# A hand-ordered attention-and-MLP kernel gets a new written order for all five engines

## Chip, cores and metric

The kernel runs on one core of a Trainium2 chip. The metric is the device time of one execution in microseconds (us). Five instruction streams run side by side and wait for each other through semaphores: TensorE (PE, matrix products and transposes), VectorE (DVE), ScalarE (ACT), GpSimd (POOL), and SyncE (SP, which only issues transfers). Each stream executes its instructions strictly in the order in which they were written.

## What is computed

Attention with four sink keys and a window of 128 keys, then a two-layer MLP with a sigmoid-gated activation:

```python
def _attn_ref(q, k, v, n_sink, window):           # (4, 8, 768, 64), n_sink 4, window 128
    scores = 1.0 / np.sqrt(D) * np.matmul(q, k.transpose(0, 1, 3, 2))
    rel = pos[:, None] - pos[None, :]
    keep = (pos[None, :] < n_sink) | ((rel >= 0) & (rel < window))
    scores = np.where(keep, scores, -1e9)
    a = np.exp(scores - np.max(scores, axis=-1, keepdims=True))
    return np.matmul(a / (np.sum(a, axis=-1, keepdims=True) + 1e-09), v)

def _moe_ref(x, w_in, w_out):                     # x (3072, 512), d_ff 2048
    h = x @ w_in
    return (h * (1.0 / (1.0 + np.exp(-1.702 * h)))) @ w_out
```

## The kernel before

The 4 x 768 queries are cut into 24 blocks of 128 tokens (all 8 heads at once). They are worked in the list ORD: first the four blocks that begin a batch (0, 6, 12, 18), which look only at their own keys, then the other twenty. "Place n" below is the position in that list: places 0 to 3 are the batch beginnings, places 4 to 23 the rest. Two places make a pair, and a pair (256 tokens) goes through the MLP together.

One place runs through these steps:

- load q, k and v of the block (lines 298 and 289). POOL issues these transfers, which also cast to 16 bits, in one queue that all loads share with the MLP weights: w_in in four quarters (line 307) and w_out in four quarters (line 316);
- transpose q and k: at places 0 to 7 by PE against the identity (line 391), evacuated by DVE or ACT; at later pairs by a DMA transpose that SP issues (line 412);
- scores on PE: at places 0 to 3 a mask is first written into PSUM by a product of the identity with `bias0` (line 438) and the scores are added (line 446); at places 4 to 7 own and previous block apart (line 446); from place 8 on both in one step (line 471). Scores against the four sinks go to `misc` (line 490), from `ksb`, the transposed sink keys;
- DVE packs own and previous block into one row of 128 keys per head (line 514), takes the maximum (526, 542, 545), subtracts (583, 598); ACT takes the exponential into `a` (616, or 569 straight out of PSUM);
- transpose `a` into `at`: at places 0 to 3 by PE (line 679), at places 4 to 23 by a DMA transpose from SP (line 717). Then POOL splits `at` by two selects: `atp`, the keys of the previous block (line 628), and `at` itself, the keys of the own block (line 622);
- values on PE (lines 738, 744, 748; two halves per place). The product with the sinks takes `vsb`, which is made once per batch out of the sink values `vsa` (a small load by SP, line 341) by a product on DVE or POOL (line 346);
- normalise on DVE into `xn` (759, 760), transpose into `xT`: at places 0 to 7 by PE (line 773), later by one DMA transpose per pair (line 786);
- MLP of the pair: eight first steps hT (line 808, eight products of 256 columns each; pair 0 in two halves of its own), the activation on ACT (838), eight second steps o (line 859, four products of 512 columns), evacuation by ACT or DVE (271, 267) and the store by SP (877).

While it waits at the beginning, PE runs products of a zero tile into `misc` (line 888). How many stand ahead of which step is said in `FILL`.

The body of the kernel only makes a list of 922 numbered operations ("plan"). The string `ORDER` then says in which order they are emitted and on which engine (P, V, A, G, S for PE, DVE, ACT, POOL, SP), and `HOME` in which ring of PSUM buffers a score, value or MLP tile lives. Costs and dependencies given to `plan.add` are notes for the search that wrote the order; the emission does not read them. What an instruction waits for follows from the data that it touches and from the buffers that it takes:

```python
    with tc.manual_schedule():
        for item in ORDER:
            op = plan.ops[int(item[:-1])]
            for n in range(FILL.get(op.seq, 0)):
                nc.tensor.matmul(misc[:, 256:512], fill[:, 0:P], fill, start=True, stop=True)
            op.emit(engines[item[-1]]) if op.many else op.emit()
```

A load on POOL has one more wait: the loads share eight semaphores in turn, so the ninth load after another is issued when that other one has landed.

Operations that are named below, by their number (the same in both kernels):

| number | what |
|---|---|
| 0, 1; 20, 21 | loads of q and k of place 0 as f32 (line 220, from SP and ACT); their casts |
| 3, 5 | the selects that make the identity (line 225) and the mask `bias0` (line 233), on POOL |
| 22 to 29 | loads of q, k, v for places 0 to 3 |
| 12 | the zeroing of `vsb` on DVE (line 251) |
| 108, 110, 114 | transposes of q and of k, scores, of place 0 |
| 580 to 595 | first steps of pair 0 |
| 101, 100, 102, 103; 104 to 107 | the loads of `vsa` for batches 1, 0, 2, 3; the products `vsb` for batches 0 to 3 |
| 236, 237, 238 and 240 | place 5: DMA transpose of `a`, the two selects, the two halves of values |
| 212, 213, 214 and 216 | the same of place 4 |
| 260, 261, 262 and 264 | the same of place 6 |
| 281 | second half of the subtraction of place 7 |
| 321, 322, 325 and 323 | the same of place 9; 310 are its scores |
| 327, 696 | the DMA transpose xT of places 8 and 9; the first MLP step that reads it |
| 357, 358, 361 | place 11: transpose, selects, first half of values |

Of the kernel before, what the change touches and what calls it, by code (L numbers as in the profile page):

```python
# [40 lines left out]
9V 2V 18V 16V 4V 13V 19V 17V 12V 23G 0S 1S 7S 22G 28G 29G 3G 15V 11V 26G 21A 20V 108P 109V 110P 5G 10V 113P 27G 132P  # L41
133A 111V 112V 114P 130P 116V 32G 24G 25G 36G 37G 131A 118A 115V 31G 117V 174P 135P 136P 137V 119A 122P 175A 176P
139V 120P 138V 121V 152P 177A 154P 179P 33G 180P 123V 153A 141A 142P 155A 140A 35G 157P 182V 181V 184A 30G 41G 40G
124P 158P 183V 185A 159V 161V 126P 143A 34G 163A 144P 160V 127V 186P 162A 145V 187V 125V 164P 188P 146P 198P 189V
147V 165A 128P 129A 148P 149V 190P 191V 168P 196P 197A 192P 166P 150P 199A 582P 193V 194P 167V 169V 170P 151A 202P
590P 171V 583A 46G 47G 50G 49G 172P 173V 586P 594P 195A 178A 39G 38G 620P 591A 587A 595A 201P 200P 222P 612P 6S 203V
220P 221A 621A 614P 613A 615A 204V 223V 205V 206V 14V 207V 134V 208V 210V 608P 588P 592P 609A 589A 593A 209V 42G 43G
52G 55G 53G 584P 246P 618P 247V 585A 8S 101S 105G 48G 56G 45G 244P 270P 245V 225P 271V 224P 228V 610P 226P 619A 268P
580P 44G 616P 269A 581A 230V 227V 229V 231V 233V 622P 617A 232V 234V 248P 249P 251V 252V 253V 596P 623A 611A 235A
# [3 lines left out]
67G 65G 61G 285G 646P 294P 296V 295V 263V 297V 647A 265V 298V 299V 636P 640P 650P 300V 301V 302V 651A 648P 649A 644P  # L53
637A 645A 638P 642P 641A 639A 59G 266P 286P 288P 643A 267V 287V 289V 303A 652P 310P 312V 313V 653P 290P 57G 86G 54G
64G 68G 291A 304S 658P 314V 315V 311P 659P 328S 316V 674P 319V 318V 660P 317V 320A 676P 661P 664P 678P 677A 675A
321S 305G 71G 364S 662A 654P 73G 329P 665A 679A 102S 331V 322G 333V 655P 668P 669A 332V 308P 334V 672P 95G 309V 330P
325P 673A 74G 335V 306P 326V 666P 70G 323P 336V 337V 667A 670P 324V 307V 63G 79G 686P 671A 338V 327S 346P 339A 687P
680P 688P 347P 348V 349V 351V 350V 656A 340S 352V 353V 106G 681P 629S 355V 354V 689P 696P 356A 690A 382P 341G 60G
697A 657S 357S 384V 385V 682P 383P 692P 683P 386V 80G 693A 400S 103S 387V 388V 389V 390V 698P 694P 699A 78G 365P
695A 684A 702P 367V 358G 369V 704P 368V 370V 391V 705A 703A 700P 344P 366P 69G 76G 66G 77G 345V 371V 701A 361P 708P  # L60
392A 362V 359P 373V 714P 360V 342P 706P 393S 343V 372V 709P 715P 374V 363S 375A 418P 685S 707A 716P 376S 420V 394G
422V 710P 421V 436S 156A 717P 423V 419P 711P 718V 424V 425V 427V 722P 663S 712A 426V 83G 720P 726P 401P 723A 721A
728P 403V 724P 402P 729A 405V 377G 107V 75G 404V 725A 406V 730P 731A 72G 82G 88G 81G 397P 398V 407V 395P 732P 733A
727A 380P 734P 742P 396V 90G 408V 410V 428A 381V 378P 379V 736P 399S 743P 409V 411A 737P 735A 412S 454P 744P 456V
429S 738P 457V 713S 455P 739P 745P 458V 459V 89G 85G 472S 460V 413G 746A 462V 461V 748P 463V 437P 749A 754P 439V
752P 755A 430G 92G 414P 753A 740A 415V 440V 442V 441V 438P 758P 762P 750P 416P 443V 84G 96G 91G 94G 445V 433P 759A
756P 417V 444V 434V 751A 763A 770P 757A 464A 431P 764P 760P 432V 446V 435S 741S 490P 447A 765P 761A 448S 491P 766P
493V 492V 494V 495V 771P 465S 496V 499V 767P 768A 508S 691S 778P 769S 449G 497V 772P 779A 498V 788P 473P 789A 466G
784P 785A 475V 476V 474P 773P 477V 478V 479V 87G 98G 99G 452P 780P 781A 482V 774A 776P 467P 790P 97G 468V 481V 782P
791A 453V 777A 480V 469P 450P 786P 451V 470V 798P 787A 471S 775S 783A 526P 500A 792P 529V 528V 799P 527P 531V 530V  # L70
793P 483A 501S 532V 800P 533V 535V 794P 484S 534V 536A 806P 795P 807A 537S 502G 509P 801P 544S 511V 485G 802V 513V
796A 512V 510P 808P 505P 809A 810P 514V 747S 818P 811A 93G 506V 486P 538G 804P 487V 503P 805A 812P 816P 504V 813A
819A 515V 516V 517V 488P 814P 826P 489V 507S 815A 817A 562P 518V 519A 565V 564V 820P 827P 563P 520S 567V 566V 568V
828P 821P 571V 569V 829P 834P 570V 572A 545P 822P 830V 521G 835A 803S 831S 842P 573S 547V 548V 823P 843A 550V 549V
524P 824A 832P 546P 551V 554V 553V 846P 574G 525V 838P 847A 833A 552V 539P 540V 541P 840P 542V 844P 839A 841A 577P
836P 837A 848P 522P 523V 555A 854P 543S 849P 855P 845A 556S 850P 719S 797S 856P 575P 851P 557G 868P 576V 852A 857P
853S 869A 862P 858A 860P 870P 560P 861A 561V 863A 578V 866P 864P 871A 558P 865A 872P 559V 867A 882P 873A 876P 825S
579S 883P 877P 874P 878P 875A 884P 879P 892P 880V 885P 881S 893A 894P 886V 888P 887S 895A 859S 890P 889A 898P 891A
896P 899A 902P 910P 897A 900P 903A 911P 901A 904P 912P 905P 916P 906P 917P 907P 913P 908V 918P 914A 919P 909S 915S
920A 921S  # L80
# [9 lines left out]
HOME = dict(x.split(":") for x in "0:own 2:pv 6:own 8:own 10:pv 12:own 16:own 17:own 19:pv 20:pv 22:mm 25:own 26:own 27:mm 28:mm 29:own 32:pv 35:pv 38:own 39:pv 41:pv 43:own 45:own 46:mm 49:mm 50:mm 52:mm 53:mm 54:own 56:pv 57:mm 59:own 60:mm 61:mm 62:mm 64:own 66:mm 67:own 69:own 70:mm 168:own 170:pv 173:pv 174:own 177:pv 178:pv 179:pv 181:own 183:own 185:pv 187:pv 188:pv 191:pv 192:own 195:pv 197:pv 203:pv 204:own".split())  # L90
# [60 lines left out]
def kernel(  # L151
# [123 lines left out]
    late = []  # L275
# [8 lines left out]
    def load_one(which, b, key, after, deps):  # L284
# [7 lines left out]
        if b in CFG["f32"]:  # L292
# [3 lines left out]
            )  # L296
        return sw(
            key, 0.88, lambda: nc.gpsimd.dma_start(buf()[:, i, w], src), 0.9,  # L298
            take=[buf], after=after, deps=deps,
        )  # L300

    for g in range(NG):
# [622 lines left out]
```

## Time and profile before

| what | us |
|---|---|
| median of 3 runs | 230.03 (230.0 to 230.13) |
| the profiled execution: its time | 229.54 |
| the profiled execution: its span, from the first to the last instruction | 227.8 |
| PE busy | 216.8 |
| DVE, ACT, POOL busy | 136.0, 127.3, 114.3 |

A row of a timeline gives the start in us, the duration in us, the engine, the line, the operation, what is written and read, and how many such instructions in a row are merged; in brackets the idle time of the engine before it and what ended it. SPq rows are the issue of a transfer, not the transfer. PE is pipelined: the duration of a row holds some 0.2 us of the last product's way through the array, so that the cost of a step is read from start to start. In the table of stretches each engine has its busy time and its number of instructions.

### The profile page before, as it was taken

To read this page: it belongs to the slowest core of one execution; us is meant where nothing else is said; L and a number is where in the kernel's file an instruction comes from. 1 tells how busy PE (TensorE), PEld (TensorE's weight loads), DVE (VectorE), ACT (ScalarE), POOL (GpSimd) and SP (SyncE) were. 2 spreads that over 40 slices of the span, in tenths; PEclk is the share of its full clock that TensorE was granted. 3 is DMA by queue.
4 is the path that set the end of the run, shared out by engine and by line. 5 is a ranking of instruction groups with operands and counts; after the bars stand their busy time and mean duration, and the time that the engine had idled before them with its cause. 6 is when DMAs were issued, how large, how long until landed. Compare 5 with 4: busy or idle time off the path is not lost.

```text
span 227.8 us, 5439 instructions
## 1 busy us (share of the span) xinstructions
PE 216.8 (95%) x2237; PEld 153.0 (67%) x2237; DVE 136.0 (60%) x334; ACT 127.3 (56%) x196; POOL 114.3 (50%) x126
## 2 busy tenths in 40 slices
PE   6789999996999999899999999999999999999994
PEld 4568998444785684585685695685695695775862
DVE  5799389674858188576875876577587751131101
ACT  2689675711584836757539359347646738441621
POOL 7995575118994594692794490570570430300000
PEclk9999999999999999999999999999999999999999
DMA  9999999999999999999999999998982703620302
GB/s 134 148 159 204 181 187 206 168 142 228 175 108 143 217 116 141 202 166 112 241 148 149 223 97 171 195 147 125 183 138 54 192 0 71 214 42 7 138 0 92
DMA packets 131992, 32.82 MB, mean 144 GB/s; under 512 B 124640, under 2 KB 129024, under 8 KB 131968
## 3 DMA queue, kind: packets, MB, share of 16 engines
q0 software_dynamic: 77024, 13.37, 77.6%
q1 hardware_dynamic: 53904, 18.85, 41.2%
q10 hardware_dynamic: 1040, 0.26, 0.5%
q8 instruction: 17, 0.28, 0.5%
q14 instruction: 7, 0.06, 0.1%
HBM read 27.36 MB, written 6.29 MB: 148 GB/s over the span
## 4 chain that ended last, share of the span: by engine, by line
PE 62%; DMA 16%; POOL 11%; issue 6%; DVE 1%; ACT 1%; POOLq 0%; SPq 0%
PE hT L808 28%; PE o L859 25%; DMA w_out<-in_moe_w_out_dram 6%; DMA w_in<-in_moe_w_in_dram 5%; POOL qkn L298 3%; DMA xT<-xn 3%; DMA at<-a 3%; POOL at L622 3%; POOL atp L628 2%; POOL v L289 2%; PE own L471 2%; PE av L744 2%; PE av L748 2%; PE av L738 1%; PE prv L471 1%
## 5 line engine op out<-in xcount | busy, mean ns | idle before, releaser
L808 PE MATMUL hT<-xT,w_in 128*128 128x256 f16 (+1 forms) x832 | 93.3, 264 | 0.9 <-DMA xT<-xn 0.9
L859 PE MATMUL o<-w_out,gT 128*128 128x512 f16 (+1 forms) x400 | 91.0, 371 | 0.0
L808 PEld LDWEIGHTS <-w_in 128*128 128x128 f16 x832 | 73.6, 98 | 13.0 <-DMA xT<-xn 1.4
L838 ACT ACTIVATE gT<-hT 128x512 f16<-128x512 f32 x96 | 54.7, 599 | 49.4 <-PE hT L808 49.0
L859 PEld LDWEIGHTS <-gT 128*128 128x128 f16 x400 | 36.8, 98 | 33.8 <-ACT gT L838 0.2
L628 POOL TENSOR_SCALAR_AFFINE_SELECT atp<-at 128x1024 f16<-128x1024 f16 x20 | 22.0, 1098 | 70.2 <-DMA at<-a 59.4
L514 DVE COPY_PREDICATED own<-later,prv 128x512 f32<-128x512 uint16 x40 | 26.5, 692 | 30.8 <-PE prv L471 25.9
L616 ACT ACTIVATE a<-e 128x1056 f16<-128x1056 f32 (+1 forms) x24 | 24.1, 1014 | 16.9 <-DVE e L598 7.1
L526 DVE TENSOR_REDUCE mx<-own 128x4 f32<-128x512 f32 x48 | 31.7, 685 | 1.6 <-PE own L446 1.1
L583 DVE TENSOR_TENSOR e<-own,mx 128x512 f32<-128x512 f32 x44 | 29.2, 684 | 0.8
L289 POOL DMA_DIRECT2D v<-in_v_dram x24 | 21.5, 899 | 3.3 <-DMA w_out<-in_moe_w_out_dram 3.3
L622 POOL TENSOR_SCALAR_AFFINE_SELECT at<-at 128x1024 f16<-128x1024 f16 x20 | 22.2, 1110 | 1.4
L298 POOL DMA_DIRECT2D qkn<-in_q_dram x23 | 20.7, 904 | 2.1 <-DMA w_in<-in_moe_w_in_dram 1.6
L298 POOL DMA_DIRECT2D qkn<-in_k_dram x23 | 20.8, 906 | 1.7 <-POOLq L906 0.8
L760 DVE TENSOR_TENSOR xn<-av,rcp 128x256 f16<-128x256 f32 x48 | 20.4, 425 | 1.7
L271 ACT COPY osb<-o 128x512 f32<-128x512 f32 (+1 forms) x18 | 10.0, 560 | 19.4 <-PE o L859 18.9
L759 DVE RECIPROCAL rcp<-av 128x4 f32<-128x4 f32 x48 | 8.5, 177 | 19.2 <-PE av L748 19.1
L744 PE MATMUL av<-v,at 128*128 128x65 f16 x192 | 16.9, 194 | 1.0 <-POOL at L622 0.7
L744 PEld LDWEIGHTS <-at 128*128 128x128 f16 x192 | 14.1, 98 | 5.2 <-POOL atp L628 2.0
L267 DVE COPY osb<-o 128x512 f32<-128x512 f32 x7 | 4.8, 690 | 19.8 <-PE o L859 19.5
L748 PE MATMUL av<-v,atp 128*128 128x65 f16 x160 | 15.0, 194 | 0.0
L838 ACT ACT_TABLE_LOAD x10 | 12.8, 1283 | 0.2
(62 smaller groups left out, 167.0 us busy)
## 6 DMA issues: line engine op xcount, KB each, us to landing
out_dram<-osb SPq DMA_DIRECT2D x23, 256.0 KB, 2.5
v<-in_v_dram POOLq DMA_DIRECT2D x24, 128.0 KB, 4.8
qkn<-in_k_dram POOLq DMA_DIRECT2D x23, 128.0 KB, 5.3
qkn<-in_q_dram POOLq DMA_DIRECT2D x23, 128.0 KB, 5.2
w_in<-in_moe_w_in_dram POOLq DMA_DIRECT2D x4, 512.0 KB, 10.1
w_out<-in_moe_w_out_dram POOLq DMA_DIRECT2D x4, 512.0 KB, 12.6
at<-a SPq DMA_TRANSPOSE x20, 4.7
rawq<-in_q_dram SPq DMA_DIRECT2D x1, 256.0 KB, 3.9
```

Source lines behind the costliest of these rows:

```text
L289: return sw(key, 0.88, lambda: nc.gpsimd.dma_start(v65[:, b, :, 0:D], src), 1.0, deps=[z_1] + deps, after=after)
L298: key, 0.88, lambda: nc.gpsimd.dma_start(buf()[:, i, w], src), 0.9,
L514: nc.vector.copy_predicated(out=own[l](), mask=later.unsqueeze(1).to_broadcast((P, 4, P)), data=prv[l]())
L526: lambda l=l, own=own, small=small, r=r: nc.vector.tensor_reduce(out=small[:, l], in_=own[l](), axis=AX.X, op=ALU.max, negate=r == 0),
L583: nc.vector.tensor_tensor(out=e32()[:, 512 * l : 512 * l + 512].rearrange("p (j s) -> p j s", j=4), in0=own[l](), in1=small[:, l].unsqueez ...
L616: nc.scalar.activation(out=a16()[:, lo:hi], in_=e32()[:, lo:hi], func=AF.Exp, scale=factor)
L622: nc.gpsimd.affine_select(out=dst()[:, lo : lo + n], in_=at()[:, lo : lo + n], pattern=[[0, n], [1, P]], compare_op=ALU.is_ge, fill=0.0, b ...
L628: nc.gpsimd.affine_select(out=dst()[:, lo : lo + n], in_=at()[:, lo : lo + n], pattern=[[0, n], [-1, P]], compare_op=ALU.is_gt, fill=0.0, ...
L744: nc.tensor.matmul(av()[:, j], ato()[:, c], v65[:, b, h], start=(r == 0), stop=(r == 0))
L808: nc.tensor.matmul(ht()[:, n], w_in16[:, c, bass.ts(f, P)], xt[g]()[:, tok, c], start=(c == 0), stop=(c == 3))
L838: lambda fs=fs, cols=cols, gt=gt, ht=ht: nc.scalar.activation(out=gt()[:, fs[0] : fs[-1] + 1, cols], in_=ht(), func=AF.Gelu_apprx_sigmoid),
L859: nc.tensor.matmul(po(), gt()[:, F, bass.ts(t, P)], w_out16[:, F, cols], start=(F == 0), stop=(F == NF - 1))
```

## The change

`ORDER` is a different sequence of the same 922 operations. `HOME` gives PSUM homes that fit it. Of the operations that may run on either of two engines, more evacuations of MLP output and of xT are on DVE (12 and 5, before 7 and 3), and the copies of sink keys are all on ACT; `vsb` of batch 0 is made by DVE and those of batches 1, 2 and 3 by POOL. `FILL` has 42 products where it had 45: 15 ahead of the first transposes, which had 16.

The selects 5 and 3 on POOL stand ahead of all loads (5) and behind two of them (3); before, four loads stood ahead of 3 and five ahead of 5. The order of the loads is another one. `vsa` of batch 0 (100) is issued by SP ahead of the transpose of place 4 (212), before behind it.

The other edits are notes for the search: three costs, one lateness, and one dependency of the loads on the mask.

```diff
 ORDER = """
-9V 2V 18V 16V 4V 13V 19V 17V 12V 23G 0S 1S 7S 22G 28G 29G 3G 15V 11V 26G 21A 20V 108P 109V 110P 5G 10V 113P 27G 132P
-133A 111V 112V 114P 130P 116V 32G 24G 25G 36G 37G 131A 118A 115V 31G 117V 174P 135P 136P 137V 119A 122P 175A 176P
...
-630P 250P 254V 255V 258V 256V 236S 631P 624P 257V 211A 259A 274P 597P 212S 625P 272P 273P 632P 275V 100S 260S 276V
-277V 278V 279V 281V 626P 598P 280V 237G 627P 628V 292S 602P 599P 603P 213G 633P 282V 283A 604P 634A 635S 284S 600A
-601S 104V 240P 261G 238P 241V 216P 214P 239V 605P 215V 217V 242P 62G 51G 606A 262P 243A 218P 607S 293P 219V 264P 58G
...
-321S 305G 71G 364S 662A 654P 73G 329P 665A 679A 102S 331V 322G 333V 655P 668P 669A 332V 308P 334V 672P 95G 309V 330P
-325P 673A 74G 335V 306P 326V 666P 70G 323P 336V 337V 667A 670P 324V 307V 63G 79G 686P 671A 338V 327S 346P 339A 687P
...
+9V 4V 15V 5G 22G 2V 23G 3G 28G 0S 6S 1S 12V 18V 16V 13V 17V 21V 29G 110P 10V 20A 108P 24G 109A 113P 111V 27G 26G
+114P 130P 11V 116V 115V 117V 131A 132P 133A 31G 174P 36G 175V 19V 135P 176P 136P 37G 118A 119A 25G 120P 177A 179P
...
+258V 256V 257V 596P 270P 597P 631P 598P 268P 236S 211A 271A 632P 625P 269A 272P 259A 273P 276V 278V 275V 277V 100S
+212S 626P 274P 602P 627P 104V 279V 282V 633P 599P 603P 237G 628A 281V 238P 240P 213G 604P 634V 280V 214P 600A 283A
+178A 54G 48G 58G 65G 216P 260S 241V 239V 242P 605P 215V 217V 218P 292S 293P 294P 243A 219V 295V 638P 639A 297V 644P
+296V 640P 298V 645A 299V 300V 302V 641A 636P 301V 648P 649A 637A 606A 59G 63G 642P 646P 647A 62G 71G 261G 643A 51G
...
+320A 321S 305G 657S 364S 73G 74G 666P 70G 322G 676P 668P 66G 678P 60G 667A 669A 679A 156A 670P 671A 329P 332V 331V
+664P 334V 333V 330P 306P 672P 665A 686P 308P 673A 677A 674P 335V 338V 307V 309V 336V 325P 323P 680P 337V 326V 681P
+324V 346P 327S 675A 348V 339A 687P 607S 347P 349V 350V 682P 340S 688P 351V 352V 354V 683P 663S 629S 353V 355V 684A
...
 FILL = dict(
...
-108:16 110:2 174:7 154:3 144:11 164:4 128:2
+110:15 114:3 132:3 174:4 120:3 157:6 188:3 146:3 128:2
...
-            o_raw[w, b] = hw(-3000, 0.4, lambda dst=raw[w, b], src=src, e=e: e.dma_start(dst, src), 0.7, late=1.15 if w == "q" else 0.5)
+            o_raw[w, b] = hw(-3000, 0.4, lambda dst=raw[w, b], src=src, e=e: e.dma_start(dst, src), 0.7, late=1.15 if w == "q" else 0.3)
...
     o_ident = plan.add(
-        POOL, -2003, 0.35,
+        POOL, -2003, 0.3,
...
     o_bias0 = plan.add(
-        POOL, -2002, 0.35,
+        POOL, -2002, 0.3,
...
         return sw(
             key, 0.88, lambda: nc.gpsimd.dma_start(buf()[:, i, w], src), 0.9,
-            take=[buf], after=after, deps=deps,
+            take=[buf], after=after, deps=deps + [o_bias0],
         )
...
-            o_ks[bb] = plan.add({DVE: 0.5, ACT: 0.5}, K0 - 39.5, 0, sink_keys, deps=o_qkt[b] + [z_k], give=[home[b]])
+            o_ks[bb] = plan.add({DVE: 0.75, ACT: 0.5}, K0 - 39.5, 0, sink_keys, deps=o_qkt[b] + [z_k], give=[home[b]])
```

More of the change, by code (lines that the diff above doesn't have):

```diff
@@ L61 @@
[L61 to L75, printed above, removed]
@@ L81 @@
+873A 578V 557G 825S 863A 857P 870P 874P 858A 864P 871A 558P 875A 860P 868P 560P 861A 869A 866P 865A 882P 867A 876P
+883P 877P 884P 878P 885P 559V 561V 579S 859S 797S 890P 886V 879P 887S 888P 891A 880V 881S 853S 898P 889A 899A 892P
+893A 896P 897A 894P 900P 910P 895A 902P 911P 901A 904P 912P 903A 905P 913P 914A 915S 906P 916P 907P 908A 909S 917P
+918P 919P 920A 921S
 """.split()
```

47 lines of the change are left out of this document (28 added, 19 removed).

## The prediction

> **What bounds the kernel.** I read the table of stretches first, then the waits of PE, then the timelines around the gaps that these two show.
>
> ```profile
> span 227.8 us, 5439 instructions
> 40.00:50.00 10.00, 10.00 (x68) 4.67 (x66) 8.00 (x18) 4.19 (x4) 0.88 (x1) 1.00 1.99 156
> 50.00:60.00 10.00, 8.01 (x101) 5.02 (x100) 4.96 (x14) 4.51 (x6) 8.80 (x9) 1.00 1.12 213
> 80.00:90.00 10.00, 9.50 (x109) 6.52 (x107) 8.23 (x22) 5.23 (x7) 8.05 (x9) 1.00 1.57 124
> 90.00:100.00 10.00, 9.06 (x92) 6.10 (x91) 6.40 (x14) 5.71 (x8) 6.70 (x7) 1.00 1.50 198
> 210.00:220.00 10.00, 10.00 (x84) 8.07 (x83) 1.25 (x2) 4.78 (x8) 0.00 (x0) 1.00 0.21 79
> PE av L738 <- DVE vsb L346: 1.8, 1, 1.8
> PE hT L808 <- DMA xT<-xn: 0.9, 1, 0.9
> ```
>
> In a row of stretches the second number is PE's busy time. From 25 us to 220 us every stretch is full except the three shown: PE misses 1.99, 0.50 and 0.94 us, 3.4 us together. An order can't shorten the full stretches, because the work on PE is the same. So 3.4 us is what can be won after the start; the start itself, up to the first MLP step, is the other place, and there PE is "busy" largely with products of zeros.
>
> **Term 1, the start: 0 (from -0.6 to +0.6).** The named part of the change is here.
>
> ```profile
> 1.13 3.39 PE L888 MATMUL misc<-fill 128*128 128x256 f16 x16 [1.13 <-DVE fill L244]
> 1.31 1.02 POOL L298 DMA_DIRECT2D qkn<-in_k_dram  x1 [0.80 <-POOLq L906]
> 4.79 0.43 DVE L267 CAST qkn<-rawq 128x512 f16<-128x512 f32 x1
> 5.03 0.33 POOL L225 TENSOR_SCALAR_AFFINE_SELECT ident<-ident 128x128 f16<-128x128 f16 x1
> 5.41 0.38 PE L391 MATMUL tq<-ident,qkn 128*128 128x128 f16 x4 [0.90 <-POOL ident L225]
> 5.46 0.62 ACT L271 CAST qkn<-rawk 128x512 f16<-128x512 f32 x1 [2.87 <-DMA rawk<-in_k_dram]
> 6.24 0.31 POOL L233 TENSOR_SCALAR_AFFINE_SELECT bias<-bias 128x124 bf16<-128x124 bf16 x1
> 8.31 0.93 PE L888 MATMUL misc<-fill 128*128 128x256 f16 x7
> 20.79 1.06 PE L808 MATMUL hT<-xT,w_in 128*128 128x128 f16 x16
> ```
>
> The identity is done at 5.36 and the cast of q at 5.22: taking the select out of the way is worth 0.14 us at most, if q stays first. It doesn't. The new order transposes k first (110 before 108), and k arrives last: its cast can't start before 5.46 and, now on DVE (0.43), ends at 5.89. PE's first transpose moves from 5.41 to about 5.95, with q right behind it, so the scores of place 0 need about what they needed. In return the mask select (0.31) delays the first loads by as much, and the two selects together cost POOL what they cost before, so from the sixth load on nothing is shifted. I followed the new order by hand from there, step by step with the durations of the old timeline, to the first MLP step: some 20.7 us, against 20.79. I take 0. The upper bound is the first transpose's delay (5.41 to 5.95) kept to the end; no row gives a gain of its own, so the lower bound is as much on the other side, for the error of such a walk.
>
> **Term 2, 50 to 60 us: -0.3 (from -1.2 to +0.9).**
>
> ```profile
> 42.16 5.91 SPq L717 DMA_TRANSPOSE at<-a  x2
> 48.12 0.71 SPq L341 DMA_DIRECT2D vsa<-in_v_dram  x1
> 50.41 1.09 POOL L628 TENSOR_SCALAR_AFFINE_SELECT atp<-at 128x1024 f16<-128x1024 f16 x1 [8.78 <-DMA at<-a]
> 51.57 1.09 POOL L622 TENSOR_SCALAR_AFFINE_SELECT at<-at 128x1024 f16<-128x1024 f16 x1
> 53.25 1.09 POOL L628 TENSOR_SCALAR_AFFINE_SELECT atp<-at 128x1024 f16<-128x1024 f16 x1 [0.58 <-DMA at<-a]
> 53.40 1.49 DVE L346 TENSOR_TENSOR vsb<-vsa,ownm 32x520 f16<-32x520 f32 x1 [3.25 <-DMA vsa<-in_v_dram]
> 54.41 1.43 POOL L622 TENSOR_SCALAR_AFFINE_SELECT at<-at 128x1024 f16<-128x1024 f16 x1
> 54.85 1.31 SPq L717 DMA_TRANSPOSE at<-a  x1
> 54.94 0.27 PE L738 MATMUL av<-vsb,at 128*128 128x260 f16 x1 [1.75 <-DVE vsb L346]
> ```
>
> PE stands before the values of place 5 until 54.94, because `vsa` was issued at 48.12, behind two transposes that held SP for 5.91 us. In the new order 100 stands between them, so it goes out near 43.5 (42.16 and one issue of 1.31), lands 5.3 us later by the old distance (48.12 to 53.40), and `vsb` is ready near 50.3 (1.49). What is late next is the select: the first transpose is let go by the same exponential as before (ACT's table load and 235 stand behind the activation of the same step 616 or its neighbour 622), lands at 50.4 under the same traffic, and its two selects end at 52.66. The second transpose now stands behind `vsa` (0.71 more); landing again near 53.2, its selects end near 55.5, where they ended at 55.84 beside DVE's product. PE takes both halves of place 5 (0.36 each, below) and one o (0.865), comes to the values of place 4 near 54.3 and waits 1.2: it begins them at 55.5, having lost about 0.3 less than by the same point of the old order. So of the 1.99 us only 0.3 is won. Bounds: the second transpose lands 0.9 earlier or waits its full 0.71 and a little more behind `vsa`.
>
> **Term 3, 82.6 us: -0.65 (from -0.7 to 0).**
>
> ```profile
> 78.55 0.90 POOL L298 DMA_DIRECT2D qkn<-in_k_dram  x1
> 80.32 1.11 POOL L628 TENSOR_SCALAR_AFFINE_SELECT atp<-at 128x1024 f16<-128x1024 f16 x1
> 81.50 1.09 POOL L622 TENSOR_SCALAR_AFFINE_SELECT at<-at 128x1024 f16<-128x1024 f16 x1
> 82.64 0.10 PEld L744 LDWEIGHTS <-at 128*128 128x128 f16 x1 [0.70 <-POOL at L622]
> 105.10 0.87 PE hT L808 x8
> 105.97 1.73 PE o L859 x8
> 107.70 0.16 PE own L471 x2
> 108.25 2.70 PE o L859 x12
> 117.91 0.11 PE av L738
> 118.27 0.11 PE av L738
> ```
>
> The last six rows, of the chain of waits, give the price of PE's steps: hT 0.87, o 0.865 (1.73 for two), scores 0.55 (107.70 to 108.25), half of the values 0.36 (117.91 to 118.27). In the old order 6 hT, 7 o, one scores and one half of values stand between the scores and the values of place 9: 5.2 + 6.1 + 0.55 + 0.36 = 12.2 us, and PE waited 0.7 for the select. In the new order it is 8 hT, 9 o and 5 halves: 7.0 + 7.8 + 0.55 + 1.8 = 17.1 us. Three loads instead of two (two took 78.55 to 80.32, 0.885 each) stand ahead of this select (322G): 0.9 us more, against 4.9 us more work. The wait goes.
>
> **Term 4, 92.4 us: -0.8 (from -1.0 to 0).**
>
> ```profile
> 85.62 0.42 DVE L760 TENSOR_TENSOR xn<-av,rcp 128x256 f16<-128x256 f32 x1
> 86.07 6.29 DMA xT<-xn
> 87.75 1.89 PE L859 MATMUL o<-w_out,gT 128*128 128x512 f16 x8
> 92.40 1.05 PE L808 MATMUL hT<-xT,w_in 128*128 128x256 f16 x8 [0.94 <-DMA xT<-xn]
> ```
>
> The transpose xT of places 8 and 9 took 6.29 us. After the last values of the pair PE had 1 hT, 6 o and one scores ahead of the waiting step, 6.6 us; now it has 7 o and two scores, 7.2 us. That is 0.55 us more room for the same latency; the rest I expect from the loads, of which three were issued in the 2 us before 86.07 and none stands there now (66G and 60G go out right after 322G). A latency of 5.7 is enough.
>
> **Term 5, waits that the new order adds: +0.3 (from 0 to +1.4).** POOL issues eight loads (54 to 71) between the selects of places 4 and 6, where before none stood. At 0.885 that is 7.1 us, and 2.25 for the selects of 261: from 55.5 to 64.85. PE has 7 hT, one o, one half, one scores and two transposes (0.22 each, by columns at hT's price) from 214 on, 8.7 us with its own half: it arrives near 64.4 and waits 0.4. Place 7 has five loads in front, 4.4 us, just in time. At place 11 the distance from scores to values is 0.5 us shorter than before, where no wait is seen; up to 0.5 is possible. Both delays twice give the upper bound. The evacuations that move to DVE cost nothing: in the stretches shown up to 100 us DVE has 1.8 to 5 us of 10 free.
>
> **Sum.** 0 - 0.3 - 0.65 - 0.8 + 0.3 = -1.45. The profiled execution took 229.54 us, 1.7 over its span, so 228.1 for its like; the median of the runs (230.03) lies 0.5 above, which gives 228.6.
>
> **Rivals.** *The clock of PE isn't released at the start (slower).* Sixteen zero products took 3.39 us, 0.21 each, the seven at 8.31 only 0.93: less the last one's 0.2, 0.11 each. PE doubles its speed between them. The new order has 15, ends them 0.2 us earlier and then idles until 5.95 instead of 5.41. If the doubling needs the sixteenth, the start runs at half speed until PE is dense again. About 11 us of PE work (7.8 of steps, by columns at hT's price, and 29 zero products of 0.11) lie between 5.4 and 20.8, so 4.4 us are idle; at half speed the further 11 us cost 11 - 4.4 = 6.6 at worst, and half of 3.39, 1.7, if PE needs another dense run as long as the first: 230.3 at the least. It decides as soon as the zero products end before the release.
> The Trainium skill's page "TensorE: Matmul & The Clock Gate", section "Part 1: The HAM clock gate", says that about 3.4 us of sustained work releases the clock, in a window that doesn't start with the kernel. By that rule 15 products of 0.21 us, an estimate of 3.2 us, could fall short; the trace agrees in the doubling, and three runs within 0.13 us speak against a release that depends on luck.
>
> *POOL's queue of selects is the new bound.* If the second transpose lands at 54.5 rather than 53.2, everything in term 5 slides with it: terms 2 and 5 become +1.0 and +0.4, the gains of 3 and 4 remain, and the time is 230.0, no change. For it speaks that the 5.91 us of SP's two transposes were mostly one that could not get in; against it, that fewer bytes of loads are left then (one v load went behind the selects).
>
> *The change does nothing:* every late transfer is late by the traffic, and the three gaps come back elsewhere: 230.0.
>
> *More is won:* the transposes at 42 to 53 us land a microsecond earlier for the same reason; term 2 becomes -1.2 and term 5 vanishes: 227.4.
>
> **How the numbers follow.** Forecast 0.5, more won 0.15, POOL's queue 0.12, nothing 0.08, the clock 0.1, and 0.05 for another late step of the start (+1.5 and more). A measurement of this kernel can tell 0.2%, 0.46 us. Faster takes the first two and 0.02 of POOL's queue: 0.67. The same takes the rest of that and half of nothing: 0.14. Slower takes the other half, the clock and the late step: 0.19. The likeliest case alone spans 227.6 to 229.6; with more won below and POOL's queue and a late clock above, 227.0 to 230.8 leaves out less than 2 in 10.
>
> **What would show it.** The wait of the values on `vsb` is gone from PE's waits and one on POOL's selects stands near 53 to 56 us; the stretches 80 to 100 are full; the first hT starts within 0.6 us of 20.8; a new small wait on POOL near 64 us. Wrong would be: a first hT after 21.5, zero products at 0.21 us after 8 us, or a stretch after 100 us that isn't full.

## The result and the profile after

| what | before | after |
|---|---|---|
| median of four runs, us | 230.03 (230.0 to 230.13) | 227.95 (227.74 to 228.54) |
| ratio of the runs, 95% interval | 1 | 0.9921 (0.9899 to 0.9942) |
| the profiled execution: its time, us | 229.54 | 227.74 |
| its span, us | 227.8 | 226.0 |
| start of the first MLP step, us | 20.79 | 21.69 |

The kernel is 2.1 us faster; 1.4 had been forecast (228.6, with 227.0 to 230.8 around it). The page after: span, PE's busy time, and the shares of the chain of waits.

```profile
span 226.0 us, 5428 instructions
PE 219.0 (97%) x2234; PEld 153.6 (68%) x2234; DVE 141.3 (63%) x334; ACT 126.7 (56%) x195; POOL 115.4 (51%) x127
PE 89%; DVE 7%; DMA 2%; issue 1%; ACT 0%
```

PE holds 89% of the chain. The table of stretches after (PE's busy time is the second number of a row):

```profile
40.00:50.00 10.00, 10.00 (x88) 5.05 (x86) 7.11 (x15) 5.99 (x7) 0.91 (x1) 1.00 1.65 169
50.00:60.00 10.00, 9.72 (x106) 6.25 (x105) 9.12 (x20) 5.02 (x8) 9.86 (x11) 1.00 1.30 178
80.00:90.00 10.00, 10.00 (x108) 6.45 (x106) 9.13 (x23) 4.64 (x6) 4.74 (x5) 1.00 1.70 149
90.00:100.00 10.00, 9.97 (x113) 7.60 (x112) 8.41 (x18) 6.71 (x10) 7.07 (x8) 1.00 1.08 191
210.00:220.00 10.00, 10.00 (x83) 7.90 (x81) 0.59 (x1) 4.55 (x8) 0.00 (x0) 1.00 0.18 66
```

The three gaps are gone: 8.01, 9.50 and 9.06 have become 9.72, 10.00 and 9.97. That is 3.1 us, and the span is only 1.8 shorter. So something was given back, and the first row of this kind to look at is the start. PE's timeline after, with the two evacuations of place 0 (ACT for q, DVE for k):

```profile
1.13 3.38 PE L888 MATMUL misc<-fill 128*128 128x256 f16 x15 [1.13 <-DVE fill L244]
5.88 1.03 PE L391 MATMUL tq<-ident,qkn 128*128 128x128 f16 x8 [1.37 <-DVE qkn L267]
6.95 0.60 ACT L269 ACTIVATE qkT<-tq 128x512 f16<-128x512 f16 x1 [1.67 <-PE tq L391]
7.56 0.85 PE L888 MATMUL misc<-fill 128*128 128x256 f16 x3
7.58 0.42 DVE L267 COPY qkT<-tq 128x512 f16<-128x512 f16 x1 [1.28 <-ACT qkT L269]
8.34 0.61 PE L446 MATMUL own<-qkT 64*128 64x128 f16 x8
21.69 1.05 PE L808 MATMUL hT<-xT,w_in 128*128 128x128 f16 x16
```

Three zero products at 7.56 take 0.85 us; less the last one's 0.2 they follow each other at 0.21, where the old kernel's at 8.31 ran at 0.11. PE was still at half speed; the spacing of its products halves between 9.06 and 9.15 us here, and between 4.09 and 4.24 in the old kernel's profile.

To see what each stage costs whatever the order of its steps, I price PE's steps as the prediction did (hT 0.87, o 0.865, scores 0.55, half values 0.36, and by columns at hT's price for the rest: four transposes 0.22, a mask 0.43), add up what PE has passed, and take the sum from the start of the next step. What is left is the time lost so far; the zero products count as lost. The whole kernel is worth 203 us of such work. Time lost, in us, when so much work has been passed:

| work passed | 7.7 (first MLP step) | 34 | 42 | 64 | 71 | 76 | 203 |
|---|---|---|---|---|---|---|---|
| before | 12.97 | 14.32 | 16.90 | 17.19 | 18.00 | 19.26 | 20.80 |
| after | 13.98 | 15.31 | 16.07 | 16.32 | 16.65 | 16.78 | 19.09 |
| difference | +1.01 | +0.99 | -0.83 | -0.87 | -1.35 | -2.48 | -1.71 |

The mark 34 lies before the values of place 5, 42 behind the first scores of place 8, 64 to 71 hold the values of place 9 and 71 to 76 the first step that reads xT of places 8 and 9. Between 34 and 42 the new order loses 0.76 instead of 2.58, at place 9 0.33 instead of 0.81, at xT 0.13 instead of 1.26, and behind 76 it loses 2.31 instead of 1.54, in pieces of 0.2 us at most. Such pieces don't show in the table of stretches, where a row holds some 0.2 us of the last product's way and bridges them: a stretch that reads 10.00 can still lose time.

### The profile page after: what moved, and what is told of

Its sections match the earlier page's. It is cut to its first block, busy times and chain, and to the rows that moved or that the text cites. A ratio compares the mean times of both kernels' runs of the same rounds, so it can differ in the third digit from the quotient of the medians.

```text
span 226.0 us, 5428 instructions
## 1 busy us (share of the span) xinstructions
PE 219.0 (97%) x2234; PEld 153.6 (68%) x2234; DVE 141.3 (63%) x334; ACT 126.7 (56%) x195; POOL 115.4 (51%) x127
## 3 DMA queue, kind: packets, MB, share of 16 engines
HBM read 27.36 MB, written 6.29 MB: 149 GB/s over the span
## 4 chain that ended last, share of the span: by engine, by line
PE 89%; DVE 7%; DMA 2%; issue 1%; ACT 0%
PE hT L808 38%; PE o L859 35%; PE own L471 2%; PE av L744 2%; DMA rawk<-in_k_dram 2%; PE av L738 2%; DVE mx L526 2%; PE av L748 2%; PE tq L391 2%; PE prv L471 2%; DVE e L583 1%; PE own L446 1%; PE tx L773 1%; PE misc L490 1%; DVE xn L760 1%; DVE own L514 1%
## 5 line engine op out<-in xcount | busy, mean ns | idle before, releaser
L808 PE MATMUL hT<-xT,w_in 128*128 128x256 f16 (+1 forms) x832 | 92.1, 264 | 0.0
L838 ACT ACTIVATE gT<-hT 128x512 f16<-128x512 f32 x96 | 55.4, 597 | 52.5 <-PE hT L808 52.0
L628 POOL TENSOR_SCALAR_AFFINE_SELECT atp<-at 128x1024 f16<-128x1024 f16 x20 | 22.5, 1127 | 64.2 <-DMA at<-a 54.2
L289 POOL DMA_DIRECT2D v<-in_v_dram x24 | 21.5, 904 | 1.4 <-DMA w_out<-in_moe_w_out_dram 1.4
L271 ACT COPY osb<-o 128x512 f32<-128x512 f32 (+1 forms) x13 | 7.2, 553 | 18.2 <-PE o L859 12.7
L267 DVE COPY osb<-o 128x512 f32<-128x512 f32 x12 | 8.2, 687 | 9.3 <-PE o L859 9.2
```

The source lines that it names most:

```text
L628: nc.gpsimd.affine_select(out=dst()[:, lo : lo + n], in_=at()[:, lo : lo + n], pattern=[[0, n], [-1, P]], compare_op=ALU.is_gt, fill=0.0, ...
L808: nc.tensor.matmul(ht()[:, n], w_in16[:, c, bass.ts(f, P)], xt[g]()[:, tok, c], start=(c == 0), stop=(c == 3))
L838: lambda fs=fs, cols=cols, gt=gt, ht=ht: nc.scalar.activation(out=gt()[:, fs[0] : fs[-1] + 1, cols], in_=ht(), func=AF.Gelu_apprx_sigmoid),
```

## The experiments

Each is one edit of the new or the old kernel. They ran on other chips of the same kind, each group beside the kernel before, whose runs there lay between 228.9 and 231.6 us; a difference of 0.3 us in the medians can't be told there, so the verdicts rest on the profiles, one execution of each kernel.

**Is the clock at the start a matter of the fifteenth or sixteenth zero product?**

e1_fill16, the new kernel:

```diff
-110:15 114:3 132:3 174:4 120:3 157:6 188:3 146:3 128:2
+110:16 114:3 132:3 174:4 120:3 157:6 188:3 146:3 128:2
```

> One zero product more ahead of the first transposes, 16 as in the old order. In the new kernel the 15 end by 4.30 us, and the transposes of place 0 then start at 5.88 with 0.107 us from one to the next (0.055 before), up to 9.15 us: half speed. Theory 'count' (the release needs the 16th product): the transposes from 5.88 on are 0.055 apart, the first MLP step starts near 21.0 instead of 21.69 and the time is 227.3. Theory 'idle gap' (the release came, and 1.6 us without work lost it): 0.107 apart as before, first MLP step near 21.7, time 227.95 as the new kernel. Theory 'order' (the loss of the start is the evacuation of k behind that of q, and the clock costs nothing): first MLP step within 0.2 of 21.7 whatever the spacing.

Its first rows:

```profile
1.12 3.60 PE L888 MATMUL misc<-fill 128*128 128x256 f16 x16 [1.12 <-DVE fill L244]
5.91 1.03 PE L391 MATMUL tq<-ident,qkn 128*128 128x128 f16 x8 [1.19 <-DVE qkn L267]
```

Sixteen products take 3.60 here and took 3.39 in the old kernel: all at 0.21, and the eight transposes behind them again 1.03. The first MLP step starts at 21.84, the time is 227.98 (0.9914, 0.9891 to 0.9936, of the kernel before). "Count" falls; these are the numbers of "idle gap".

e3_before15, the old kernel:

```diff
-108:16 110:2 174:7 154:3 144:11 164:4 128:2
+108:15 110:2 174:7 154:3 144:11 164:4 128:2
```

> The old order with 15 zero products ahead of the first transposes instead of 16; idle time ahead of them 1.1 us (4.30 to 5.41), as against 0.93 in the old kernel and 1.57 in the new one. Theory 'count': transposes from 5.41 on are 0.107 apart, first MLP step at 21.2 or later instead of 20.79, time 230.5 or more. Theory 'idle gap': 0.055 apart, first MLP step at 20.8, time 230.03 as before.

```profile
1.13 3.25 PE L888 MATMUL misc<-fill 128*128 128x256 f16 x15 [1.13 <-DVE fill L244]
5.45 0.38 PE L391 MATMUL tq<-ident,qkn 128*128 128x128 f16 x4 [1.07 <-POOL ident L225]
```

With fifteen the old kernel's transposes run at full speed (0.38 for four, as before), first MLP step 20.82; the time is 230.63 (1.002, 0.9996 to 1.0045). The number of products decides nothing.

e2_fill26, the new kernel with `110:26`:

> 26 zero products ahead of the first transposes instead of 15, so that PE has next to no idle time ahead of them: at 0.21 us up to the fifteenth and 0.11 behind it they end near 5.5 us. Theories 'count' and 'idle gap' both say: transposes 0.055 apart, first MLP step near 21.0, time 227.2 to 227.4; if the doubling fails to come by then (all at 0.21, end near 6.7), the first transposes are 0.8 later and the time is 228.5 or more. Theory 'order': first MLP step within 0.2 of 21.7, time 227.95.

The spacing halves at 6.0 us, in the midst of products that had run without a break since 1.13; 23 had been done at half speed, so the transposes begin at 6.35 rather than 5.88. The first MLP step starts at 21.17, the time is 227.69 (0.9901, 0.9877 to 0.9924). The release had been expected near 4.1, so "idle gap", by which it came and was lost again, doesn't explain this run: here it came late without a gap.

e4_evac_dve, the new kernel:

```diff
-... 110P 10V 20A 108P 24G 109A 113P 111V 27G 26G
+... 110P 10V 20A 108P 24G 109V 113P 111V 27G 26G
```

> The new kernel with q of place 0 evacuated by DVE instead of ACT, so that q (0.42) and k (0.42) follow each other on one engine, as in the old order; k's evacuation stood at 7.58 to 8.00 behind ACT's of q (6.95 to 7.55). Theory 'order': k is done near 7.8, and the scores of place 0 start at 8.1 to 8.3 instead of 8.34, first MLP step 21.5, time 227.8. Theory 'clock': the three zero products ahead of the scores, at half speed, end only at 8.2, so the scores stay at 8.3 and the first MLP step at 21.7; time 227.95.

Half speed up to 10.4 us; from the first transpose to the scores it takes 2.46 us (5.79 to 8.25), as in the new kernel (5.88 to 8.34), and the first MLP step starts at 21.89. Time 228.09 (0.9917, 0.9889 to 0.9946). At half speed the evacuations are not what the scores wait for.

What settled it came with kernels made for other questions. e6 below has the new kernel's start to the letter, e8 the old one's, and their clocks fell the other way round. PE's first rows of e6 (new start), then of e8 (old start):

```profile
5.90 0.62 PE L391 MATMUL tq<-ident,qkn 128*128 128x128 f16 x8 [1.63 <-DVE qkn L267]
7.66 0.40 PE L446 MATMUL own<-qkT 64*128 64x128 f16 x8 [0.36 <-DVE qkT L267]
20.72 1.05 PE L808 MATMUL hT<-xT,w_in 128*128 128x128 f16 x16
```

```profile
1.13 3.59 PE L888 MATMUL misc<-fill 128*128 128x256 f16 x16 [1.13 <-DVE fill L244]
5.42 0.58 PE L391 MATMUL tq<-ident,qkn 128*128 128x128 f16 x4 [0.69 <-POOL ident L225]
21.96 1.06 PE L808 MATMUL hT<-xT,w_in 128*128 128x128 f16 x16
```

The new start at full speed reaches the first MLP step at 20.72, the old start at half speed at 21.96. So an early and a late release both occur in both orders; a late one costs 1.0 to 1.2 us of the start, and with an early one the new order costs nothing (20.72 against 20.79). Whether the orders share the same odds isn't shown: with 15 or 16 zero products ahead, full speed had come by 5.9 us in four of five profiles of the old order (before, e3, e7, e9; not e8) and in one of five of the new one (e6; not after, e1, e4, e5), and the new order leaves PE idle longer ahead of the first transposes (1.4 us before them in the rows above, 0.9 in the old kernel).

**What ends the stretch of 50 to 60 us?**

e7_vsa_ahead, the old kernel:

```diff
-... 259A 274P 597P 212S 625P 272P 273P 632P 275V 100S 260S 276V
+... 259A 274P 597P 100S 212S 625P 272P 273P 632P 275V 260S 276V
```

> The old kernel with 100 ahead of 212 on SP, and nothing else of the change. The step of the prediction: the wait of the values on vsb (1.75 us) is gone, the transposes land at about 50.4 and 53.2 to 53.9 as before, and the selects of place 4 (end 55.5 to 56.2) make PE wait about 1.2: 0.3 us are won (the loss between 52 and 60 us of the span, 2.6 in the old kernel, falls to 2.3). Rival: the transposes land a microsecond or more earlier without the small load's place behind them, and 1.2 us or more are won, as in the new kernel.

From its timeline, and the first row of its table of PE's waits:

```profile
51.55 1.16 DVE L346 TENSOR_TENSOR vsb<-vsa,ownm 32x520 f16<-32x520 f32 x1 [1.28 <-DMA vsa<-in_v_dram]
54.78 1.09 POOL L622 TENSOR_SCALAR_AFFINE_SELECT at<-at 128x1024 f16<-128x1024 f16 x1
55.94 0.20 PE L744 MATMUL av<-v,at 128*128 128x65 f16 x1 [1.32 <-POOL at L622]
```

```profile
PE av L744 <- POOL at L622: 2.8, 4, 1.3
```

The wait on `vsb` is gone and PE waits 1.32 for the second select of place 4 instead, nearly the 1.2 of the prediction. It gains nothing: at 42 us of work 16.93 us are lost against 16.90; the time is 230.07 (1.0006, 0.9982 to 1.0031). In the old order the selects are next in line.

e6_vsa_behind, the new kernel:

```diff
-... 275V 277V 100S
-212S 626P 274P 602P 627P 104V ...
+... 275V 277V 212S
+100S 626P 274P 602P 627P 104V ...
```

> The new kernel with 100 (vsa of batch 0) behind 212 (the transpose of place 4) on SP, as in the old order; 212 held SP for 2.71 us in the new kernel and 4.27 in the old one. Theory 'vsa alone': vsa is issued near 47.7 instead of 44.97, vsb is done near 54.6 instead of 51.9, and PE waits 1.4 us for it at the values of place 5 (which start at 53.15 in the new kernel); time 1.0 to 1.4 longer. Theory 'backlog': the small load lands within 4 us too, vsb is done near 53 and PE waits less than 0.3; time unchanged.

```profile
50.74 1.29 DVE L346 TENSOR_TENSOR vsb<-vsa,ownm 32x520 f16<-32x520 f32 x1 [0.98 <-DMA vsa<-in_v_dram]
53.88 0.27 PE L738 MATMUL av<-vsb,at 128*128 128x260 f16 x1 [1.18 <-DVE e L583]
```

`vsa` is issued at 47.67 and lands 3 us later, so `vsb` itself is in time for the first half (PE at 52.18). But DVE stood 0.98 for it, and the second half waits 1.18 for a subtraction that is queued behind `vsb`. Time 228.2 (0.9928, 0.99 to 0.9957). Neither theory had that: what is late is not `vsb` but DVE's queue.

e5_v_back, the new kernel:

```diff
-... 623A 616P 624P 43G 44G 45G 247V 233V ...
+... 623A 616P 624P 43G 44G 45G 48G 247V 233V ...
-178A 54G 48G 58G 65G 216P 260S ...
+178A 54G 58G 65G 216P 260S ...
```

> The new kernel with one load (48, v of place 6) put back ahead of the selects of places 5 and 4, behind load 45, as in the old order. Theory 'backlog' (the transposes of places 5 and 4 land when the loads issued ahead of them have landed; the old kernel had 33 loads ahead, the last landing at 53.0 beside a second transpose at 53.19, the new one 32 and landings at 49.03 and 50.60): landings near 50.2 and 52.5, the second select pair ends near 55, PE waits 0.3 to 0.8 us on POOL's selects for the values of place 4. Theory 'vsa alone' (the move of the small load is what won the stretch): landings within 0.5 of 49.0 and 50.6 and no wait on the selects.

The transposes land at 49.74 and 50.76 instead of 49.03 and 50.60, 0.7 and 0.2 us later where "backlog" asked for 1.2 and 1.9, and PE does not wait on the selects: that load doesn't explain the old kernel's 50.34 and 53.19. Whether it costs anything isn't shown, since in the six other kernels with the new order the two land at 48.6 to 50.2 and at 50.3 to 51.8. Time 228.0 (0.9909, 0.9879 to 0.9938).

With e6 in mind, DVE's rows of the new kernel, PE's halves of place 5 and its first transpose of `xn`:

```profile
50.25 1.09 POOL L622 TENSOR_SCALAR_AFFINE_SELECT at<-at 128x1024 f16<-128x1024 f16 x1
50.63 1.26 DVE L346 TENSOR_TENSOR vsb<-vsa,ownm 32x520 f16<-32x520 f32 x1
53.01 0.68 DVE L583 TENSOR_TENSOR e<-own,mx 128x512 f32<-128x512 f32 x1
53.15 0.27 PE L738 MATMUL av<-vsb,at 128*128 128x260 f16 x1
53.61 0.68 DVE L267 COPY osb<-o 128x512 f32<-128x512 f32 x1
53.74 0.27 PE L738 MATMUL av<-vsb,at 128*128 128x260 f16 x1
54.20 0.68 DVE L583 TENSOR_TENSOR e<-own,mx 128x512 f32<-128x512 f32 x1
56.04 0.40 PE L773 MATMUL tx<-ident,xn 128*128 128x128 f16 x4 [0.20 <-DVE xn L760]
```

`vsb` ends at 51.89 and the transpose of `xn` starts at 56.04, 4.15 us later. In all eight kernels with the new order this distance is 4.14 to 4.16 us, while `vsb` ends anywhere from 50.80 to 52.62: DVE's chain behind `vsb` (maximum, subtraction, evacuation, subtraction, normalisation) is what PE meets there. At 42 us of work the loss is the end of `vsb` less 35.8 us in all eight, wherever their starts lay. The evacuation in this chain (634) ran on ACT in the old order. The same rows of e2:

```profile
50.12 0.68 DVE L346 TENSOR_TENSOR vsb<-vsa,ownm 32x520 f16<-32x520 f32 x1
50.28 1.48 POOL L622 TENSOR_SCALAR_AFFINE_SELECT at<-at 128x1024 f16<-128x1024 f16 x1
54.95 0.40 PE L773 MATMUL tx<-ident,xn 128*128 128x128 f16 x4
```

Here `vsb` began ahead of the select and took 0.68, and the select was the one that became longer; everything behind it is 1.1 us earlier.

**Is it the load beside xT, or the longer piece of PE work?**

e8_load_behind, the old kernel:

```diff
-... 307V 63G 79G 686P 671A ...
+... 307V 63G 686P 671A ...
-... 690A 382P 341G 60G
+... 690A 382P 341G 79G 60G
```

> The old kernel with one load (79, issued at 86.03, landed at 92.27) moved behind the next first select (341), so that the transpose xT of places 8 and 9, issued at 86.07 and landed at 92.36, has no load issued right ahead of it. Theory 'backlog': it lands about when the load before it lands, 89.8 to 90.5, PE's wait of 0.94 us on it at 92.4 is gone, and the time is 0.5 to 0.9 less. Rival 'work on PE alone' (only the longer piece of PE work between the values and that step removes the wait): landing within 0.5 of 92.4, wait 0.9, time 230.05.

The transfers of e8 between 84 and 93 us (number, median from issue to landing), and PE's one long wait behind them:

```profile
xT<-xn SPq DMA_TRANSPOSE x1, 5.0
```

```profile
101.82 0.19 PE L744 MATMUL av<-v,at 128*128 128x65 f16 x1 [0.92 <-DMA v<-in_v_dram]
```

xT takes 5.05 us instead of 6.29 and lands at 91.18, between the values of the two theories, and the loss between 71 and 73 us of work falls from 1.12 to 0.02: the load did it, with PE's work unchanged. But load 60, the v of place 10, now stands right behind 79: issued at 95.39 (95.36 before) it lands at 101.78 instead of 100.60, and PE, which comes a microsecond earlier, pays 0.92 there. So the 0.5 to 0.9 us less did not come; the time stays: 229.99 (1.0003, 0.998 to 1.0026).

**The named part alone, and a start that is late for certain.**

e9_selects, the old kernel:

```diff
-9V 2V 18V 16V 4V 13V 19V 17V 12V 23G 0S 1S 7S 22G 28G 29G 3G 15V 11V 26G 21A 20V 108P 109V 110P 5G 10V 113P 27G 132P
+9V 2V 4V 5G 3G 18V 16V 13V 19V 17V 12V 23G 0S 1S 7S 22G 28G 29G 15V 11V 26G 21A 20V 108P 109V 110P 10V 113P 27G 132P
```

> The old kernel with the named part of the change alone: the selects that make the identity and the mask stand ahead of all loads on POOL, their zeroings ahead on DVE. The prediction's step: the first transposes wait for the cast of q instead of the identity and start 0.14 us earlier (5.27 instead of 5.41), all loads are issued 0.6 us later up to the fifth, nothing later moves, and the time is 230.0. Rival: the loads of places 1 to 3, 0.6 us later, hold the start up, and the first MLP step is 0.3 to 0.6 us later.

```profile
4.65 0.90 POOL L298 DMA_DIRECT2D qkn<-in_k_dram  x1
4.91 0.90 DVE L267 CAST qkn<-rawq 128x512 f16<-128x512 f32 x1
5.86 0.40 PE L391 MATMUL tq<-ident,qkn 128*128 128x128 f16 x4 [1.14 <-DVE qkn L267]
```

The identity is there early, but the fourth load, 0.6 us later than before, now lies over the cast of q, which takes 0.90 instead of 0.43: PE starts at 5.86, later than the 5.41 of the old kernel, and reaches the first MLP step at 21.59, at full speed. Time 229.97 (0.9989, 0.9971 to 1.0007). The 0.14 us at the front did not come, the loss of 0.8 at the first MLP step is more than the rival had, and the time is as before: the named part alone brings nothing.

e12_old_nofill is the old kernel without the sixteen zero products (`108:16` taken out of `FILL`), e11_new_nofill the new one without its fifteen.

> The old kernel without the zero products ahead of the first transposes: release after 9 us, first MLP step at 21.9 or later instead of 20.79. Theory 'absorbed' (the old order stands 50 to 60 us for loads and transposes whose time doesn't hang on PE's start, so PE's late start only shortens its wait there): time within 0.4 of the kernel before. Rival 'passes through': 1.1 us or more longer, 231.1 or more.

> The new kernel without the zero products ahead of the first transposes, so that the clock is late in every run: release after 9 us, first MLP step at 21.9 or later. Theory 'passes through' (the new order has no wait on transfers between 25 and 220 us, so a late start is paid in full at the end): time 228.2 to 229.2, as much over 227.95 as the first MLP step is over 21.7, and a narrower spread than the new kernel's.

e12 runs at half speed until 10.9 us and reaches the first MLP step at 22.09, 1.30 later than the old kernel. At 42 us of work it has lost 16.51 us, less than the old kernel's 16.90, and its span is 227.5 against 227.8: in this execution the late start is absorbed. Its median, 230.76 (1.0024, 0.9991 to 1.0056), lies between the two theories: six of its twelve runs took 229.2 to 230.3, as "absorbed" has it, and six 231.3 to 232.6, as "passes through" has it. Only one of the first kind was profiled, so what delays the others stays open. e11 reaches the first MLP step at 22.99, 1.30 later than the new kernel, and has lost 16.80 at 42, 0.73 more than the new kernel. The rest of its loss is a new wait:

```profile
PE own L471 <- DMA qkT<-qkn: 1.3, 1, 1.3
```

Its time is 229.4 (0.9939 to 0.9985 of the kernel before, at 0.9962): 1.4 over the new kernel, just above the range expected, for a wait that was not, and with no narrower spread.

**The best of both.** e10_best, the new kernel with `110:22` and `109V`:

> The new kernel with 22 zero products ahead of the first transposes (they end near 5.8 us at half speed, or near 5.0 if the clock is released at 4.1) and q of place 0 evacuated by DVE. Theory 'window' (the clock is released at the end of a stretch of some 3.4 us in which PE was busy nearly throughout, and these stretches have no fixed place against the start of the kernel: releases at 4.1 and 6.06 us are seen where PE was kept busy, at 9.15 to 10.2 where the zero products ended at 4.3 and the stretch that follows held 1.1 to 1.6 us of idle time): release at 6.8 us at the latest, scores of place 0 near 7.8, first MLP step 20.6 to 21.1, time 226.6 to 227.4. Rival 'chance alone' (the number of zero products doesn't matter): release after 9 us in one of two profiles, time 227.95.

```profile
1.12 4.38 PE L888 MATMUL misc<-fill 128*128 128x256 f16 x22 [1.12 <-DVE fill L244]
6.03 0.62 PE L391 MATMUL tq<-ident,qkn 128*128 128x128 f16 x8 [0.53 <-DVE qkn L267]
20.55 1.05 PE L808 MATMUL hT<-xT,w_in 128*128 128x128 f16 x16
```

The spacing halves at 4.9 us, the scores start 1.46 us behind the first transpose (1.76 in e6, with q on ACT), and the first MLP step at 20.55 is the earliest of all. Time 227.64 (0.9877, 0.985 to 0.9904), above the 226.6 to 227.4 expected. Its interval overlaps the new kernel's, so a further gain isn't shown. Nor is "chance alone" excluded: e2 and e10 are one profile each, and five of the ten with 15 or 16 products were at full speed by 5.9 us too. The profile says why it can be only small:

```profile
50.90 1.00 DVE L346 TENSOR_TENSOR vsb<-vsa,ownm 32x520 f16<-32x520 f32 x1 [1.32 <-DMA vsa<-in_v_dram]
52.91 0.20 PE L744 MATMUL av<-v,at 128*128 128x65 f16 x1 [0.60 <-POOL at L622]
```

PE comes 1.1 us earlier to the values of place 5 and waits there: on the select, and on DVE, which stood 1.32 for `vsa`. Time lost, in us, of the kernels that bear on this:

| kernel | at 7.7 | at 34 | at 42 | at 76 | at 203 |
|---|---|---|---|---|---|
| before | 12.97 | 14.32 | 16.90 | 19.26 | 20.80 |
| e7 (old, vsa ahead) | 12.98 | 14.45 | 16.93 | 19.40 | 21.71 |
| e8 (old, load behind; late clock) | 14.14 | 15.66 | 16.81 | 18.21 | 20.82 |
| e12 (old, no zero products) | 14.27 | 15.61 | 16.51 | 18.95 | 20.49 |
| after (late clock) | 13.98 | 15.31 | 16.07 | 16.78 | 19.09 |
| e10 (new, 22 products, 109V) | 12.84 | 14.17 | 16.08 | 16.61 | 18.92 |
| e6 (new, vsa behind) | 13.01 | 14.35 | 16.21 | 16.93 | 19.55 |
| e2 (new, 26 products) | 13.46 | 14.80 | 14.98 | 15.51 | 18.65 |
| e5 (new, one load back; late clock) | 14.01 | 15.35 | 15.63 | 16.23 | 18.55 |

A start that differs by 1.3 us among the old kernels differs by 0.4 at 42, and the latest has lost least. Among the new ones the earliest start (e10) and a late one (after) have lost the same at 42; of these only e2 and e5, whose `vsb` was done by 51.44, get below.

## Why the prediction was right, and where it was wrong

**The bound.** Right: the three gaps were what could be won, 3.1 of their 3.4 us are closed, and the stretches behind 100 us are full in both. But full was read as without loss, and it isn't (term 5).

**Term 1, the start (0, from -0.6 to +0.6).** The profiled start is 0.90 later, outside the bounds, and at 21.69 the first MLP step shows the sign that the prediction had named for being wrong (after 21.5). Still the walk was right: with the clock released early the same instructions reach the first MLP step at 20.72 (e6), where the walk by hand had 20.7. What failed is the treatment of the clock. The rival tied the release to the sixteenth product; e1 and e3 show both combinations that it excludes. It priced the late clock at 1.7 us of the time or more, and in the profiled execution it cost 1.0 at the start and nothing at 42 us of work (16.07 lost there, with an early clock 16.08 in e10 and 16.21 in e6). And the argument against chance, "three runs within 0.13 us speak against a release that depends on luck", fails in its inference: the old order takes up a start that is 1.2 us late in the wait at 50 to 60 us (e8), so such times need not show the release: e8's profiled execution took 229.55 with a late clock, the old kernel's 229.54 with an early one. The profile of a single execution was taken for the kernel's start, when it was one draw of it. The Trainium skill's page "TensorE: Matmul & The Clock Gate", section "Part 1: The HAM clock gate", has the window running freely, and says that the same kernel varies with its phase at the start; the releases here at 4.0 (e6), 4.1 to 4.2, 4.9, 6.0, 9.1 and 10.9 us agree with that, and the prediction had set that rule too low.

**Term 2, 50 to 60 us (-0.3).** The move of `vsa` did what was said, and in the old order the next thing late is the select, at the predicted price (e7: 1.32 against 1.2). In the new order it isn't: "what is late next is the select" is the step that failed. The selects end by 54.0 instead of the predicted 55.5, since the first transpose, issued 1.2 us later than in the old kernel, lands 1.3 earlier (49.03 against 50.34). In their place stands DVE's chain behind `vsb`. Terms 1 and 2 together were put at -0.3 and are -0.83 at 42 us of work, well inside the bound of -1.2. Why the transposes are faster was not isolated by an edit, but the fourteen profiles of both orders agree on one thing, the number of loads still under way when the first of them was issued (three in the new kernel, eight in the old one). With three it took 3.9 to 5.7 us, with four or five 6.2 to 6.8, with six or seven 7.0 to 8.1, with eight 8.2 to 8.9.

**Term 3, place 9 (-0.65).** -0.48 by the work from 64 to 71, with the wait gone: the result fits. The longer piece of work before the values was the reason given; no experiment isolates it, so the cause is argued and not shown.

**Term 4, xT (-0.8).** -1.13, a little over the bound of -1.0: right in kind. The prediction gave 0.55 us of room to PE's work and left the rest to the loads; e8 takes one load away from beside the transpose, without any work on PE being moved, and the loss of 1.12 goes, so the loads alone are enough.

**Term 5, new waits (+0.3).** Neither of the two came: place 6 starts at 64.24 without a wait, and place 11 shows none. Instead 0.77 more is lost behind 76 us of work, in pieces under 0.2 us that no table of waits names. Laid against the price from start to start, most of it, 0.68, is six pauses of PE of 0.05 to 0.19 us; apart from the steps into and out of scores, where both orders pay alike, the old kernel has none over 0.02 there. Four of the six, 0.52 together, end within 0.06 us of the end of a DVE instruction. The longest:

```profile
93.64 0.68 DVE L267 COPY osb<-o 128x512 f32<-128x512 f32 x1
94.38 0.82 PE L808 MATMUL hT<-xT,w_in 128*128 128x256 f16 x6
```

This evacuation (690) ran on ACT in the old order; the other three DVE instructions belong to the normalisation, and the two pauses left (0.16) end behind an activation on ACT. So the sentence "the evacuations that move to DVE cost nothing" is a step that failed: it was read from DVE's free share of each stretch, and what counted was when DVE came to the instruction that PE needed. No run puts the evacuation back on ACT, so its price is read from this trace alone. The sign and about the size of the term were right, by luck, since the places were wrong.

**The sum.** -1.45 predicted, -1.8 in the span, with +1.0 and -1.8 hidden inside the first two terms, each of which is mostly the other's mirror: what the late clock costs at the start is not waited for at 50 us. That the total came so near is luck in this: the start, term 2 and term 5 each went otherwise than worked out.

## What to carry to other kernels

A start is only worth shortening if nothing behind it waits for something that has its own clock. Before pricing an edit at the front, ask whether the first wait on a transfer further back would take up the difference; here it hid about 1 us in either direction in the executions profiled (not in all: half of e12's runs were longer), and let a release that varies look fixed. And when a wait is removed, look at the queue of the engine that held it: the product that was late was in time, the work queued behind it was not.

## What the hardware showed that had not been expected

- PE's clock is released at different moments: the spacing of its products halved at 4.0 us (e6), 4.1 to 4.2 (the old kernel), 4.9 (e10), 6.0 (e2), 9.1 (the new kernel), 10.5 (e8) and 10.9 (e12, without products at the front). Where PE was kept busy from 1.13 us past 5.4, in e2 and e10, it came by 6.0. The granted clock in the tables of stretches is 1.00 all the same, as in the rows above, so that only the spacing of the products shows it.
- A transpose that SP issued right behind a load landed with it in both places looked at: issued at 86.07, 0.04 behind a load that landed at 92.27, it landed at 92.36; issued at 69.96, 0.10 behind one that landed at 76.16, at 76.22. Where no load was under way the transposes of `a` late in the old kernel took 3.30 and 3.36 us (issued at 158.34 and 161.74).
- DVE and POOL lengthen each other. `vsb` took 0.68 when it began ahead of a select and 1.26 when a select was running, up to 0.55 beyond that select's end (51.34 and 51.89). In the six kernels with the new order in which it began 0.2 us or more before the end of a select it ended 0.54 or 0.55 behind that select, whether it took 0.77 or 1.29, and the select after it ended 0.96 behind `vsb` in all eight; the select behind the early `vsb` took 1.48 instead of 1.09. A cast of f32 took 0.90 instead of 0.43 under the issue of a load. The Trainium skill's page "SBUF — State Buffer", section "SBUF: two separate sides", says that DVE and GpSimd share a pair of ports under an exclusive lock, by which the one that starts first holds the other up, for a DVE operation with two SBUF inputs when the other one reads SBUF; the rows of `vsb` and the selects agree.
